# Adjacent heads in the two partition halves, with whole-tile loads of q, k and v and first-layer weights loaded by blocks of 32 partitions

## The chip, the cores and the metric

The kernel runs on one core of one Trainium2 chip. The metric is the device time of one execution in microseconds (us), lower is better. Engine names are those of the profile: PE is TensorE (matmul), PEld its weight loads, DVE VectorE, ACT ScalarE, POOL GpSimd, SP SyncE. SP, ACT and POOL can issue DMAs.

## What is computed

Attention with normalised q and k, and behind it a two-layer MLP with a leaky activation.

```python
# q, k, v: (8, 12, 448, 64) float32;  g_q, g_k: (64,)
def rmsnorm(x, g):
    return x / np.sqrt(np.mean(x * x, axis=-1, keepdims=True) + 1e-06) * g
q_n, k_n = rmsnorm(q, g_q), rmsnorm(k, g_k)
scores = q_n @ k_n.transpose(0, 1, 3, 2) / np.sqrt(64)
attn = np.exp(scores - scores.max(axis=-1, keepdims=True))
attn = attn / (attn.sum(axis=-1, keepdims=True) + 1e-09)
attn_out = attn @ v
x = attn_out.transpose(0, 2, 1, 3).reshape(8 * 448, 12 * 64)   # 3584 x 768
h = x @ w_in                                                   # w_in 768 x 2048
g = np.maximum(h, 0) + alpha * np.minimum(h, 0)
out = g @ w_out                                                # w_out 2048 x 768
```

## The kernel before

**Steps.** The 12 heads of a batch are laid out as two halves of the 128 partitions: g = 0 on partitions 0 to 63, g = 1 on 64 to 127. A partition holds J = 7 consecutive rows of the sequence for each head (64 x 7 = 448). A step y handles two heads of each half, so four heads; three steps (G = 3) make a batch, and 24 steps the kernel. Before the change half g holds heads 6g to 6g + 5, so that the four heads of a step are two neighbours and two other neighbours six heads away.

**Load and normalise.** `load_qk(y)` loads q and k of a step into two float32 tiles `nat` of 128 partitions x 2 heads x 448 values, each with one DMA for each half (L125). All go through SP, but for the second halves of steps 0 and 1, which ACT issues. For step 1 a copy on ACT into the tile (L123) keeps the load back. Steps 2, 5 and 8 load into a part of the tile `arena`. `square` (POOL, L180), `reduce` (DVE, L188) and `root` (ACT, L198 and L199) give the reciprocal root mean square, `scale` (DVE in the first steps, POOL from the k of step 3 on, L208) multiplies it in and makes a float16 tile `qs`. `follow` is a one-element copy on POOL (L282) that makes POOL wait for a scaling on DVE. `turn`, `turn_one` and, from step 7 on, `turn_dma` (SP, L307) transpose to `qT` and `kT`; PE does it in the early steps (L333). Step 0 is done in pieces (the `part_` functions), head by head for the squares of q. Ahead of its transposes PE runs a fixed number of dummy matmuls (`spin`, L765).

**Attention.** `score` (PE, L360) makes a tile of scores, `soft` (ACT, L374) exponentiates it to `expT`; `den` sums over keys by matmuls with ones, `attv` multiplies with v. The float16 tile `vt` holds v of a batch, loaded by `load_v` with one casting DMA for each half from POOL's queue (L134). In `attv` the 64 values of a head are taken as two sets of 32 columns: before the change the even and the odd ones. So block i of the transposed attention output `xT[:, g, i]` holds, on four groups of 32 partitions, 32 values each of four heads (i = 0 the even, i = 1 the odd ones of the first two steps), and for the third step 32-value groups of its two heads (i = 2).

**MLP.** `up` (PE, L499) multiplies a 128-column tile of `w_in_sb` with `xT`, six blocks (2 halves x 3) for each of 16 tiles; ACT (L539) and DVE (L543) apply the activation, and `down` (L561) and the `quad` functions (L626), which do four products with seven by sums and differences of blocks, make the output. `w_in_sb[:, block, :]` must hold the rows of w_in in the order in which `xT` holds its values. `load_w_in(c)` casts a quarter of the columns (512) for the blocks i = 0 and 1 with one DMA for each half, each over 128 partitions (L144), and, for even c, two quarters of the blocks i = 2 with two DMAs of 64 partitions (L151). It is called four times, at fixed places of POOL's queue among the squares and scalings of steps 2 to 5. `load_w_out` is called four times behind it (L158).

**Order.** The order of the work on each engine is written out by hand: a list of bursts of score tiles, with the functions `at` and `after` that put a job before or behind a burst, and a table that spreads `up`, `down` and `quad` units over the bursts. Nothing is reordered at run time: an engine that waits holds up all that is queued behind it. Waits for tiles are put in by the framework from what each instruction reads and writes.

Of the kernel before, what the change touches and what calls it, by code (L numbers as in the profile page):

```python
# [21 lines left out]
def kernel(  # L22
# [12 lines left out]
    nc = tc.nc  # L35
# [4 lines left out]
    J = S // 64  # L40
    HH = H // 2
    G = HH // 2
# [5 lines left out]
    FB = DF // 4  # L48
# [15 lines left out]


    q4, k4, v4 = (
        t.rearrange("b (g h) (p j) d -> b g p h (j d)", g=2, j=J) for t in (q, k, v)
    )
    out4 = out.rearrange("(b p j) m -> b j p m", b=B, j=J)

# [13 lines left out]
    w_in_sb = cst.tile([128, KM, DF], FP16, name="w_in_sb", tag="w_in_sb")  # L84
# [13 lines left out]
    def lent(start, size):  # L98

        return arena[:, start // 4 : (start + size) // 4]  # L100
# [5 lines left out]
    nat, sqs, qs, ss_t, rr_t, qkT, vt, xT = {}, {}, {}, {}, {}, {}, {}, {}  # L106
    SRC = {"q": q4, "k": k4}
# [4 lines left out]
    def load_qk(y, hold=False):  # L112
        b, i = divmod(y, G)
        for nm in "qk":
            if y in (2, 5, 8):
                t = lent(HB + "qk".index(nm) * NB4, NB4).rearrange(
                    "p (h j d) -> p h j d", h=2, j=J
                )
            else:
                t = ld.tile([128, 2, J, D], FP32, name="nat", tag="nat", bufs=4)  # L120
            if hold and nm == "q":

                nc.scalar.copy(out=t[:, 0, 0, 0:1], in_=expb)  # L123
            for g in range(2):
                (nc.scalar if y < 2 and g else nc.sync).dma_start(  # L125
                    out=t[ds(64 * g, 64)].rearrange("p h j d -> p h (j d)"),
                    in_=SRC[nm][b, g, :, ds(2 * i, 2)],
                )
            nat[y, nm] = t

    def load_v(b):
        t = att.tile([128, HH, J, D], FP16, name="vt", tag="vt", bufs=1)
        for g in range(2):
            nc.gpsimd.dma_start(  # L134
                out=t[ds(64 * g, 64)].rearrange("p h j d -> p h (j d)"), in_=v4[b, g]
            )
        vt[b] = t

    def load_w_in(c):

        src = moe_w_in[:, ts(c, FB)].rearrange("(g r) f -> g r f", g=2)
        dst = w_in_sb[:, :, ts(c, FB)].rearrange("p (g i) f -> p g i f", g=2)
        for g in range(2):
            nc.gpsimd.dma_start(  # L144
                out=dst[:, g, 0:2], in_=src[g, :256].rearrange("(p e) f -> p e f", e=2)
            )
        if c % 2 == 0:
            src = moe_w_in[:, ts(c // 2, 2 * FB)].rearrange("(g r) f -> g r f", g=2)
            dst = w_in_sb[:, :, ts(c // 2, 2 * FB)].rearrange("p (g i) f -> p g i f", g=2)
            for e in range(2):  # L150
                nc.gpsimd.dma_start(  # L151
                    out=dst[ds(64 * e, 64), :, 2],
                    in_=src[:, 256:].rearrange("g (p e) f -> e p g f", e=2)[e],
                )

    def load_w_out(c):
        oh, half = divmod(c, 2)
# [192 lines left out]
    def pre(ys):  # L350
        return len(ys) == 1 and ys[0] >= PRE and ys[0] % G == G - 1
# [27 lines left out]
    def over_keys(accs, ys, weights):  # L379

        heads = [(y, par, c) for y in ys for c in range(3 - len(ys)) for par in range(2)]
        for j in range(J):
            for n, (y, par, c) in enumerate(heads):
                for g in range(2):
                    nc.tensor.matmul(  # L385
                        out=accs[g][ds(32 * n, 32), :S],
                        lhsT=weights(g, y, par, c, j),
                        rhs=expT[y][ds(64 * g, 64), j, par, :],
                        start=(j == 0),
                        stop=(j == J - 1),  # L390
                    )

    def halved(ys):

        return len(ys) == 1 and ys[0] not in (2,)
# [48 lines left out]
    def attv(ys, half, spare=False, jobs=(), put=None, early=False):  # L444

        b, i = divmod(ys[0], G)
        v2 = vt[b].rearrange("p h j (d e) -> p h j d e", e=2)

        def weights(g, y, par, c, j):
            h = 2 * (y - G * b) + par  # L450
            return v2[ds(64 * g, 64), h, j, :, half if len(ys) == 2 else c]

        if half:
            av, accs = None, [psf.tile([128, 512], FP32, name="avb", tag="mm") for _ in range(2)]
        else:
            pool, tag = (pss, "sc") if spare else (psa, "acc")
            av = pool.tile([128, 2, 512], FP32, name="av", tag=tag)
            accs = (av[:, 0], av[:, 1])
        over_keys(accs, ys, weights)
        for f in jobs:  # L460
            f(ys)
        if b not in xT:
            xT[b] = att.tile([128, 2, G, S], FP16, name="xT", tag="xT")
        x, r = xT[b][:, :, i + half, :], rden[ys]
        if half:
            for g in range(2):
                nc.vector.tensor_mul(out=x[:, g], in0=accs[g][:, :S], in1=r[:, g])
        else:
            parts = [(x, av[:, :, :S], r)]
            if halved(ys):  # L470
                parts = [
                    (x[ds(64 * e, 64), :, c], av[ds(64 * e, 64), :, c], r[ds(64 * n, 64)])
                    for n, c in enumerate(ts(n, S // 2) for n in range(2)) for e in range(2)
                ]
            if put is not None:
                soon = 2 if early else 0
                muls(parts[:soon])
                put.append((muls, (parts[soon:],)))
            else:
                muls(parts)  # L480

    def muls(parts):
        for x, av, r in parts:
            nc.vector.tensor_mul(out=x, in0=av, in1=r)  # L484
# [10 lines left out]
    def up_part(hT, b, ft, lo, hi):  # L495

        for i in range(lo, hi):
            for g in range(2):
                nc.tensor.matmul(  # L499
                    out=hT[:, :S],  # L500
                    lhsT=w_in_sb[:, g * G + i, ts(ft, 128)],
                    rhs=xT[b][:, g, i, :],
                    start=(i == 0 and g == 0),
                    stop=(i == G - 1 and g == 1),
                )
# [274 lines left out]
    while m < NG * J or steps:  # L780
        n = len(bursts)
        while steps:
            ys, values = steps[0]
# [18 lines left out]
        while len(bursts[n]) < limit and m < NG * J:  # L802
            y, j = divmod(m, J)
# [29 lines left out]
    for y in range(G, NG):  # L833

        early = y < G + 2
        if early:
            n = turn_at[y - 1] + 1
        elif y == G + 2:
            n = den_at[G - 1]
        elif y == 2 * G:  # L840
            n = turn_at[y] - 4
        elif y % G == 1:
            n = den_at[y - 4] - 1 - pre((y - 2,))
        elif y % G:
            n = den_at[y - G] - pre((y - G,))
        else:
            n = av_at[y - 4]
        low = y > 3 * G + 1
        if low:
            nexts[root_at[y - 2]] = y  # L850
        elif y in (3 * G - 1, 3 * G):

            after(den_at[G] - (y < 3 * G), load_qk, y)
        else:
            at(n - (6 if early or y % G == G - 1 and pre((y - G,)) else 3 if y == 2 * G else 4 if y < 3 * G else 5), load_qk, y)
# [9 lines left out]
        if y == 3 * G:  # L865
            after(n, *jobs[n].pop()[:1], y, "k")
        roots[root_at[y]] = y
    at(av_at[G] - 6, load_v, 1)
    for b in range(2, B):
        after(av_at[G * b - 1] + 1, load_v, b)  # L870
# [116 lines left out]
    for n, g in enumerate((g_q, g_k)):  # L987
        for h in range(2):
            nc.gpsimd.dma_start(
                out=rows[NF + n : NF + n + 1, ds(64 * h, 64)], in_=g.unsqueeze(0)  # L990
# [12 lines left out]
    for h in range(2):  # L1003
# [13 lines left out]
        out=gain, in0=cols[:, NF : NF + 1], in1=cols[:, NF + 1 : NF + 2]  # L1017
# [3 lines left out]
    part_copy("q", full, nc.vector)  # L1021
    part_copy("k", lo, nc.vector)
    load_v(0)
    part_scale("k", hi, J - K0, nc.vector)
    follow(0, "k")
# [22 lines left out]
    for n in range(NB):  # L1048
# [6 lines left out]
        for t in first_tiles:  # L1055
            if t == (0, J - 2):
                spin(1)
            elif t == (1, J - 3):
                spin(2, False)
            elif t == (1, J - 2):  # L1060
                spin(1, False)
            elif t == (0, J - 1):
                turn_one(1, "q")
            elif t == (1, 0):
                turn_one(1, "k")
            elif t == (1, J - 1):
                turn(2)
            score(*t)
            if n == den_at[G - 1] - 1 and t == tiles[-1]:
                begin(0)  # L1070
                begin(1)
            elif lead and t == tiles[0]:
                soft(*t)
                den(dens[n])
                attv(avs[n], 0, True, (log, invert))
            elif lead and t == tiles[1]:
                begin(2)
# [26 lines left out]
        if n in avs and not lead and not sums:  # L1104

            for half in (1, 0) if avs[n] == (0, 1) else (0,):
                attv(avs[n], half)
# [11 lines left out]
        if n in roots:  # L1119
            y = roots[n]  # L1120
# [43 lines left out]
        for k, (f, a) in enumerate(gaps[n]):  # L1164
# [5 lines left out]
            else:  # L1170
                f(*a, spare)
                done += 1
                if n in jobs and not (lead and done < 5) and (
                    n < av_at[2 * G - 1] or done % 2
                ):
                    g, c = jobs[n].pop(0)
# [3 lines left out]
                while late and done == late[0][0]:  # L1180
                    _, g, c = late.pop(0)
# [51 lines left out]
```

## Time and profile before

| | |
|---|---|
| Median of 3 runs | 416.07 us (415.39 to 417.27) |
| The profiled execution | 418.46 us, its span 416.7 us |
| PE busy | 398.8 us (96%) |
| POOL busy | 255.8 us (61%) |
| DVE, ACT busy | 266.0 us, 257.6 us |
| DMA queue q1 (SP) | 53520 packets, 39.54 MB |
| DMA queue q0 (POOL) | 13472 packets, 11.81 MB |
| DMA queue q10 (ACT) | 976 packets, 1.31 MB |
| HBM read, written | 45.62 MB, 11.01 MB |

| DMA issues | count | KB each | us from issue to landing, median |
|---|---|---|---|
| q halves into nat, SP | 40 | 224.0 | 4.5 |
| k halves into nat, SP | 40 | 224.0 | 5.4 |
| q and k halves into arena, SP | 6 and 6 | 224.0 | 8.1 and 8.3 |
| q and k halves into nat, ACT | 2 and 2 | 224.0 | 5.2 and 6.8 |
| v halves, POOL | 16 | 336.0 | 8.4 |
| w_in, POOL | 12 | 256.0 | 9.4 |
| w_out, POOL | 4 | 768.0 | 10.5 |

A row of a timeline has the start in us from the span's start, the duration, the engine, the line, the operation, what is written and read, the count, and in brackets the idle time of the engine ahead of it with what ended it. "issue" in brackets is a wait that the profile shows no releaser for. POOLq and SPq are the issuing sides of these engines. In a DMA view, the share of a queue is the time that its packets took, as a share of 16 DMA engines over the stretch; it can pass 100% where packets overlap on an engine. Bytes are those written, so a casting load from float32 to float16 reads twice as many.

### The profile page before, as it was taken

What the parts mean: (1) busy time and instruction counts of PE and PEld (TensorE: products, weight loads), DVE (VectorE), ACT (ScalarE), POOL (GpSimd) and SP (SyncE); (2) the same over time, 40 slices, a digit from 0 to 9 for tenths busy, and PEclk for the clock granted to TensorE, in tenths of its full rate; (3) what the DMA queues carried; (4) which work ended last, traced back from release to release, by engine and by line L of the source; (5) the groups of instructions that cost most, each with busy time, mean ns of one, the idle gap of its engine ahead of it and who ended that gap; (6) DMA issues with size and microseconds to landing.
All of it is one profiled execution on the core that took longest, in us unless ns stands there. A gap on an engine that the chain in (4) does not pass through costs nothing.

```text
span 416.7 us, 11767 instructions
## 1 busy us (share of the span) xinstructions
PE 398.8 (96%) x5055; PEld 208.2 (50%) x5055; DVE 266.0 (64%) x420; ACT 257.6 (62%) x390; POOL 255.8 (61%) x180
## 2 busy tenths in 40 slices
PE   8698999999998999989999999999999999999996
PEld 3344445444455445544455445544555445655664
DVE  3875775476564575794788685958576755465322
ACT  4896687667845686565775787775656784135110
POOL 6689695669587985787094748386633507400870
PEclk9999999999999999999999999999999999999999
DMA  8999999973927496929946596369522800320133
GB/s 179 231 237 232 182 214 150 227 189 67 177 44 189 105 162 106 173 62 191 154 69 165 116 202 143 86 147 194 98 56 52 138 3 21 77 58 0 37 95 96
DMA packets 68019, 53.39 MB, mean 128 GB/s; under 512 B 35568, under 2 KB 67456, under 8 KB 67968
## 3 DMA queue, kind: packets, MB, share of 16 engines
q1 hardware_dynamic: 53520, 39.54, 45.0%
q0 software_dynamic: 13472, 11.81, 19.4%
q10 hardware_dynamic: 976, 1.31, 1.3%
q8 instruction: 39, 0.64, 0.7%
q14 instruction: 12, 0.10, 0.1%
HBM read 45.62 MB, written 11.01 MB: 136 GB/s over the span
## 4 chain that ended last, share of the span: by engine, by line
PE 46%; DVE 7%; DMA 1%; ACT 0%; issue 0%; SPq 0%; DVEq 0%
PE hT L499 14%; PE hTa L499 7%; PE qx L626 5%; PE oq L626 3%; PE sc L360 3%; PE qc L626 3%; PE av L385 2%; PE qz L626 2%; PE oqm L626 2%; DVE ss L188 1%; PE avb L385 1%; PE oqa L626 1%; DVE xT L484 1%; PE dn L385 1%; DVE kT L318 1%; DMA out_dram<-osb 1%
## 5 line engine op out<-in xcount | busy, mean ns | idle before, releaser
L374 ACT ACTIVATE expT<-sc 128x896 f16<-128x896 f32 x168 | 147.8, 914 | 53.2 <-PE sc L360 53.0
L499 PE MATMUL hT<-xT,w_in_sb 128*128 128x448 f16 x546 | 113.6, 353 | 3.5 <-issue 2.3
L499 PEld LDWEIGHTS <-w_in_sb 128*128 128x128 f16 x768 | 72.9, 98 | 77.9 <-issue 13.5
L543 DVE TENSOR_TENSOR gT<-hT,gT 128x448 f16<-128x448 f32 x91 | 56.7, 623 | 41.3 <-ACT gT L539 40.5
L208 POOL TENSOR_TENSOR qs<-nat,rr 128x896 f16<-128x896 f32 x36 | 61.0, 1713 | 34.8 <-issue 22.3
L539 ACT ACTIVATE gT<-hT,cols 128x448 f16<-128x448 f32 x90 | 57.1, 635 | 36.1 <-PE hT L499 35.9
L180 POOL TENSOR_TENSOR sq<-nat 128x896 f32<-128x896 f32 x32 | 53.6, 1683 | 39.7 <-DMA nat<-in_q_dram 30.4
L360 PE MATMUL sc<-qT,kT 64*32 64x448 f16 (+1 forms) x1092 | 52.9, 356 | 4.4 <-ACT expT L374 1.9
L626 PEld LDWEIGHTS <-gT 128*128 128x128 f16 x352 | 33.5, 98 | 26.8 <-issue 5.7
L499 PE MATMUL hTa<-xT,w_in_sb 128*128 128x448 f16 x210 | 45.5, 352 | 0.0
L188 DVE TENSOR_REDUCE ss<-sq 128x14 f32<-128x896 f32 (+1 forms) x37 | 38.5, 1053 | 4.4 <-POOL sq L180 4.3
L484 DVE TENSOR_TENSOR xT<-av,rden 64x448 f16<-64x448 f32 (+1 forms) x37 | 27.2, 734 | 13.5 <-PE av L385 5.5
L539 ACT ACTIVATE gT<-hTa,cols 128x448 f16<-128x448 f32 x35 | 22.3, 637 | 18.9 <-PE hTa L499 18.9
L543 DVE TENSOR_TENSOR gT<-hTa,gT 128x448 f16<-128x448 f32 x35 | 21.8, 624 | 18.1 <-ACT gT L539 18.0
L360 PEld LDWEIGHTS <-kT 64*32 64x32 f16 (+1 forms) x1092 | 15.6, 93 | 35.1 <-issue 29.3
L561 PE MATMUL op<-w_out_sb,gT 128*128 128x384 f16 x160 | 27.6, 327 | 1.0 <-issue 1.0
L385 PEld LDWEIGHTS <-vt 64*32 64x32 f16 x1344 | 20.2, 92 | 13.5 <-issue 4.3
L561 PEld LDWEIGHTS <-gT 128*128 128x128 f16 x192 | 17.9, 98 | 14.8 <-issue 3.8
L614 POOL TENSOR_TENSOR gs<-gT 128x1024 f16<-128x1024 f16 x3 | 6.4, 2123 | 30.4 <-DVE gT L543 28.1
L385 PE MATMUL av<-expT,vt 64*32 64x448 f16 x896 | 24.3, 350 | 0.3 <-DVE osb L674 0.3
L622 POOL TENSOR_TENSOR gT<-gT 128x1024 f16<-128x1024 f16 x11 | 23.4, 2126 | 0.0
L626 PE MATMUL qx<-w_out_sb,gT 128*128 128x384 f16 x120 | 20.8, 326 | 1.0 <-DVE rden L428 1.0
(148 smaller groups left out, 492.6 us busy)
## 6 DMA issues: line engine op xcount, KB each, us to landing
out_dram<-osb SPq DMA_DIRECT2D x107, 96.0 KB, 3.0
nat<-in_q_dram SPq DMA_DIRECT2D x40, 224.0 KB, 4.5
nat<-in_k_dram SPq DMA_DIRECT2D x40, 224.0 KB, 5.4
vt<-in_v_dram POOLq DMA_DIRECT2D x16, 336.0 KB, 8.4
w_in_sb<-in_moe_w_in_dram POOLq DMA_DIRECT2D x12, 256.0 KB, 9.4
w_out_sb<-in_moe_w_out_dram POOLq DMA_DIRECT2D x4, 768.0 KB, 10.5
arena<-in_q_dram SPq DMA_DIRECT2D x6, 224.0 KB, 8.1
arena<-in_k_dram SPq DMA_DIRECT2D x6, 224.0 KB, 8.3
```

The costliest lines, as they stand in the source:

```text
L180: nc.gpsimd.tensor_mul(out=sqf[:, c], in0=src[:, c], in1=src[:, c])
L188: nc.vector.tensor_reduce(out=o[:, c], in_=sqs[y, nm][:, c], axis=AXIS_X, op=ALU.add)
L208: eng.tensor_mul(out=t.rearrange("p j h d -> p h j d"), in0=nat[y, nm], in1=rr_t[y][:, "qk".index(nm)].unsqueeze(3).broadcast_to((128, 2, ...
L360: nc.tensor.matmul(out=sc[ds(64 * g + m * c, m), par, :S].rearrange("p (j c) -> p j c", j=J), lhsT=kT[ds(64 * par, 64), j, g, ts(c, m)], r ...
L374: nc.scalar.activation(out=expT[y][:, j], in_=scs[y, j][:, :, :S], func=AF.Exp, scale=QK_SCALE, bias=EXP_BIAS,)
L385: nc.tensor.matmul(out=accs[g][ds(32 * n, 32), :S], lhsT=weights(g, y, par, c, j), rhs=expT[y][ds(64 * g, 64), j, par, :], start=(j == 0), ...
L484: nc.vector.tensor_mul(out=x, in0=av, in1=r)
L499: nc.tensor.matmul(out=hT[:, :S], lhsT=w_in_sb[:, g * G + i, ts(ft, 128)], rhs=xT[b][:, g, i, :], start=(i == 0 and g == 0), stop=(i == G ...
L539: nc.scalar.activation(out=g, in_=hT[:, :S], func=AF.Copy, scale=alpha_sb[:, ft : ft + 1])
L543: nc.vector.tensor_max(out=g, in0=hT[:, :S], in1=g)
L561: nc.tensor.matmul(out=op[:, :OH], lhsT=gT[:, ft, ts(tile % J, 128)], rhs=w_out_sb[:, ft, ts(oh, OH)], start=(ft == 0), stop=(ft == NF - 1),)
L626: nc.tensor.matmul(out=bank[:, c], lhsT=g[:, ft], rhs=v[:, ft, c], start=(first and ft == 0), stop=(ft == HF - 1), skip_group_check=True,)
```

## The change

Half g now holds the heads of parity g: the four heads of a step are four neighbours in memory, and partition and half together are one dimension of 128 with one stride. With that, q and k of a step are one DMA each over 128 partitions, all on SP's queue (q of step 0 in two, one for each head index), and v of a batch is one DMA. `attv` takes the first and the second 32 values of a head and no longer the even and odd ones. The rows of w_in follow: `w_in_sb` holds blocks 0 to 3 (i = 0 and 1 of both halves) and 4, 5 (i = 2), which `block_of` numbers; for each group of 32 partitions one DMA loads its rows, four for blocks 0 to 3 of each quarter of the columns, and four for blocks 4 and 5 of each half of the columns: 24 DMAs in all where there were 12.

```diff
@@ -64,7 +64,7 @@
 
 
     q4, k4, v4 = (
-        t.rearrange("b (g h) (p j) d -> b g p h (j d)", g=2, j=J) for t in (q, k, v)
+        t.rearrange("b (h g) (p j) d -> b (g p) h (j d)", g=2, j=J) for t in (q, k, v)
     )
     out4 = out.rearrange("(b p j) m -> b j p m", b=B, j=J)
 
@@ -121,37 +121,34 @@
             if hold and nm == "q":
 
                 nc.scalar.copy(out=t[:, 0, 0, 0:1], in_=expb)
-            for g in range(2):
-                (nc.scalar if y < 2 and g else nc.sync).dma_start(
-                    out=t[ds(64 * g, 64)].rearrange("p h j d -> p h (j d)"),
-                    in_=SRC[nm][b, g, :, ds(2 * i, 2)],
-                )
+            o = t.rearrange("p h j d -> p h (j d)")
+            for h in range(2) if (y, nm) == (0, "q") else (slice(0, 2),):
+                nc.sync.dma_start(out=o[:, h], in_=SRC[nm][b, :, ds(2 * i, 2)][:, h])
             nat[y, nm] = t
 
     def load_v(b):
         t = att.tile([128, HH, J, D], FP16, name="vt", tag="vt", bufs=1)
-        for g in range(2):
+        nc.gpsimd.dma_start(out=t.rearrange("p h j d -> p h (j d)"), in_=v4[b])
+        vt[b] = t
+
+    def block_of(g, i):
+        return 2 * g + i if i < 2 else 4 + g
+
+    def load_w_in(c):
+
+        src = moe_w_in[:512].rearrange("(n x p) f -> n p x f", n=4, p=32)
+        for n in range(4):
             nc.gpsimd.dma_start(
-                out=t[ds(64 * g, 64)].rearrange("p h j d -> p h (j d)"), in_=v4[b, g]
-            )
-        vt[b] = t
-
-    def load_w_in(c):
-
-        src = moe_w_in[:, ts(c, FB)].rearrange("(g r) f -> g r f", g=2)
-        dst = w_in_sb[:, :, ts(c, FB)].rearrange("p (g i) f -> p g i f", g=2)
-        for g in range(2):
-            nc.gpsimd.dma_start(
-                out=dst[:, g, 0:2], in_=src[g, :256].rearrange("(p e) f -> p e f", e=2)
+                out=w_in_sb[ds(32 * n, 32), :4, ts(c, FB)], in_=src[n, :, :, ts(c, FB)]
             )
         if c % 2 == 0:
-            src = moe_w_in[:, ts(c // 2, 2 * FB)].rearrange("(g r) f -> g r f", g=2)
-            dst = w_in_sb[:, :, ts(c // 2, 2 * FB)].rearrange("p (g i) f -> p g i f", g=2)
+            w = ts(c // 2, 2 * FB)
+            src = moe_w_in[512:].rearrange("(n g e p) f -> e n p g f", n=2, g=2, e=2)
             for e in range(2):
-                nc.gpsimd.dma_start(
-                    out=dst[ds(64 * e, 64), :, 2],
-                    in_=src[:, 256:].rearrange("g (p e) f -> e p g f", e=2)[e],
-                )
+                for n in range(2):
+                    nc.gpsimd.dma_start(
+                        out=w_in_sb[ds(64 * e + 32 * n, 32), 4:, w], in_=src[e, n, :, :, w]
+                    )
 
     def load_w_out(c):
         oh, half = divmod(c, 2)
@@ -444,11 +441,11 @@
     def attv(ys, half, spare=False, jobs=(), put=None, early=False):
 
         b, i = divmod(ys[0], G)
-        v2 = vt[b].rearrange("p h j (d e) -> p h j d e", e=2)
+        v2 = vt[b].rearrange("p h j (e d) -> p h j e d", e=2)
 
         def weights(g, y, par, c, j):
             h = 2 * (y - G * b) + par
-            return v2[ds(64 * g, 64), h, j, :, half if len(ys) == 2 else c]
+            return v2[ds(64 * g, 64), h, j, half if len(ys) == 2 else c]
 
         if half:
             av, accs = None, [psf.tile([128, 512], FP32, name="avb", tag="mm") for _ in range(2)]
@@ -498,7 +495,7 @@
             for g in range(2):
                 nc.tensor.matmul(
                     out=hT[:, :S],
-                    lhsT=w_in_sb[:, g * G + i, ts(ft, 128)],
+                    lhsT=w_in_sb[:, block_of(g, i), ts(ft, 128)],
                     rhs=xT[b][:, g, i, :],
                     start=(i == 0 and g == 0),
                     stop=(i == G - 1 and g == 1),
```

## The prediction, made before the changed kernel ran

> **What bounds the kernel now.** I read the page first: which engine is full, and in which slices.
>
> ```profile
> PE 398.8 (96%) x5055; PEld 208.2 (50%) x5055; DVE 266.0 (64%) x420; ACT 257.6 (62%) x390; POOL 255.8 (61%) x180
> ...
> PE   8698999999998999989999999999999999999996
> ...
> DMA  8999999973927496929946596369522800320133
> ```
>
> TensorE (PE) is busy 398.8 of 416.7 us, so 17.9 us of idle time is all that faster transfers can give back. The windows place it: 8.35 us before 50 us (41.65 busy), 5.5 us from 50 to 400, 4.0 us behind that. DMA is dense (9) in the first seven slices of 10.4 us. In that front POOL squares and scales q and k and, between these, issues the loads of v and of the weights; so POOL's timeline comes next.
>
> ```profile
> 18.49 1.68 POOL L180 TENSOR_TENSOR sq<-arena 128x896 f32<-128x896 f32 x1
> 20.11 1.48 POOL L144 DMA_DIRECT2D w_in_sb<-in_moe_w_in_dram  x2
> 21.59 1.22 POOL L151 DMA_DIRECT2D w_in_sb<-in_moe_w_in_dram  x2
> 24.08 0.19 POOL L282 COPY mark<-qs 128x1 f16<-128x1 f16 x1 [1.27 <-DVE qs L208]
> 24.22 3.46 POOL L180 TENSOR_TENSOR arena<-nat 128x896 f32<-128x896 f32 x3
> 27.63 1.46 POOL L144 DMA_DIRECT2D w_in_sb<-in_moe_w_in_dram  x2
> 29.11 2.42 POOL L208 TENSOR_TENSOR arena<-nat,rr 128x896 f16<-128x896 f32 x1
> ...
> 45.48 3.33 POOL L208 TENSOR_TENSOR qs<-nat,rr 128x896 f16<-128x896 f32 x2 [3.34 <-ACT rr L199]
> ```
>
> POOL hardly rests from 18 us on: its slack is 1.27 us before 24.08 and 3.34 us before 45.48. The second exists because PE itself stood still; PE's timeline:
>
> ```profile
> 42.47 0.92 PE L499 MATMUL hT<-xT,w_in_sb 128*128 128x448 f16 x4 [2.34 <-issue]
> ...
> 49.29 0.95 PE L333 MATMUL tps<-ident,qs 128*128 128x128 f16 x14
> ```
>
> The 2.34 us are the longest PE stall. Nothing on chip ends it: xT was done at 39.97, and the c=0 weights had landed by 34.9. What does end near it is a block of 16,384 bytes on the instruction queue, moved from 39.70 to 41.01. Such blocks come every 252 recorded PE instructions; this one came some 200 too late by that count, and the one at 130.98 some 220, before PE's next long stall. I read both as instructions kept back by crowded DMA engines. How crowded, the DMA view of two stretches tells:
>
> ```profile
> DMA packets 290, 0.46 MB, mean 230 GB/s; under 512 B 32, under 2 KB 290, under 8 KB 290
> ...
> q1 hardware_dynamic: 288, 0.46, 107.8%
> ```
> ```profile
> q0 software_dynamic: 450, 0.50, 73.6%
> q1 hardware_dynamic: 286, 0.45, 40.5%
> ```
>
> First 12 to 14 us, where q1 (the q and k halves) runs alone: 288 packets take 107.8% of 16 engines for 2 us, 120 ns each. Then 31 to 35 us, beside the weights: 40.5% of 16 x 4 us over 286, 91 ns. Alone they are slower than in company, so the half-loads hinder one another. Single packets of 1,792 bytes span 74 ns (5th percentile) to 166 ns; at 74 ns, 16 engines would move 387 GB/s.
>
> Last, 130 to 139 us, the one place behind the front where a late load reaches PE:
>
> ```profile
> 130.30 1.68 POOL L180 TENSOR_TENSOR sq<-nat 128x896 f32<-128x896 f32 x1 [2.79 <-DMA nat<-in_q_dram]
> ...
> 133.68 3.42 PE L561 MATMUL op<-w_out_sb,gT 128*128 128x384 f16 x20 [0.99 <-issue]
> ...
> 138.19 1.11 PE L499 MATMUL hT<-xT,w_in_sb 128*128 128x448 f16 x5 [0.59 <-DVE osb L572]
> ```
>
> POOL's squares wait for q, DVE's reduction (134.03) for POOL, the xT products (135.03 to 137.55) and the osb copy stand behind it on DVE, and PE waits 0.59 us for that copy.
>
> **The change part by part.** *q and k loads.* Two DMAs of 64 partitions become one of 128. A pair is 917,504 bytes: 4.0 us at the 230 GB/s shown, 2.4 us at 387. I take the latter, since 91 ns is already seen in company; the other bound is no gain.
>
> The Trainium skill, page "SBUF — State Buffer", section "Door 1: The DMA port swizzle (why [64,N] ≈ [32,N])", says that partitions 0 to 63 reach only 8 of 16 ports, some 218 GB/s, and all 128 reach twice that. The 230 GB/s agree with it; by its 436 GB/s a pair would take an estimated 2.1 us, which leaves the sum as it is. It also speaks against the other half of the change, as 32 partitions reach 8 ports too; the trace shows the weights written at 204 GB/s on 128 partitions (56 to 60 us), so by the rule the pieces would hardly be slower.
>
> *Issues on SP and ACT.* A half-load costs SP 0.60 us with 128 runs, an output with 64 runs 0.61, so I price a whole load at 0.6 too (at most 1.2, the two it replaces). ACT loses four issues (0.63 to 0.86 us) before 5.3 us. The first q lands sooner, but no score comes sooner: PE's spins run to 9.19 and the transposes behind them set the first score at 11.04. Worth 0 on the path.
>
> *Front of POOL.* k of step 1 no longer keeps POOL back at 12.55: it starts at 11.8, behind the copy of 11.65, and all that hangs on it is 0.75 us earlier; the square of 18.49 ends near 19.35.
>
> *w_in.* 12 issues become 24. The nearest row for 32 partitions x 4 runs is L151 with as many runs (64 x 2): 0.62 us; the g loads with 16 runs took 0.49, L144 with 256 runs 0.73. I take 0.60, ends 0.49 and 0.73. Then: c=0, 8 x 0.60, ends at 24.15 (marker copy 24.3, against 24.22 before: the 1.27 us of slack and the 0.75 are used up). Squares to 27.75; c=1 (4 x 0.60 for 1.46) to 30.15; scale of k to about 31.85 (1.7, as elsewhere; in the row above DVE stretched it to 2.42). PE transposes this k from about 32.3, so nothing is lost. Squares to 35.15, c=2 to 39.95, squares to 43.3, c=3 to 45.7, scale of step 4 to 49.0. PE without its 2.34 us stall would reach step 4's transposes at 46.95, does q's, and waits for k until 49.05; before, k's seven began at about 49.77. **Front: -0.7 us.** Ends: -2.3 (0.49 us an issue: POOL in time) and +2.4 (0.73: c=0 to 25.2, c=3 to 48.8, k scaled at 52.1). What hid the old issues was POOL's slack; now it is gone, and PE's recovered time with it.
>
> *v.* One issue of 768 runs for two of 0.69: between 0.73 and the 0.94 of a w_out issue with 1,024; about 0.5 us less POOL time a batch, beside full PE: 0.
>
> *Steady stage.* From 50 to 130 us PE has no stall over 0.25 us, so there is nothing to gain. At 125.6 the pair lands (data from 127.0) by 129.8 and not 132.16: POOL's two squares end at 132.1 instead of 133.99, xT 1.8 us sooner, and the 0.59 us go; the instruction block meets 2.4 us of load and not 5, so the 0.99 goes. **-1.6 us** (ends 0 and -1.6). The stalls at 179.5 (0.98) and 186.6 (0.32) have DVE full for microseconds ahead of them: 0, ends ±1.0. At 215.5 (0.64): 0 or -0.6.
>
> *Weight layouts.* v's columns become contiguous, block numbers of w_in change: loads of vt (stride 2) take 92 ns, of contiguous kT 93, under the matmuls: 0.
>
> Sum: -0.7 - 1.6 = -2.3 us. The profiled execution took 418.46 us (span 416.7 and 1.8 around it) and becomes 416.2; the median of the runs, 2.4 us lower, becomes 413.8, 0.55% less. About 0.5%, 2.1 us, is what a measurement of this kernel can tell from no change, so this forecast lies just beyond it.
>
> **The rivals.** *One: POOL's eight slots, slower.* The DMA records show POOL's loads on eight semaphores (111 to 118) in turn, and on SP that a ninth load waits for the first: the k load of 6.95 starts when semaphore 104 fills at 6.94, 0.7 us after the issue before it. With 24 weight loads, c=1 waits for the landing of c=0's first four. It decides once a landing exceeds 8.4 us (27.75 - 19.35). Now they take 8.0 to 12.7. At 11.0, the L151 median: c=1 issued to 32.75, c=2 43.75, c=3 51.15, scale 54.5, so +4.8: 420.9; at 9.4, +1.6. Against it: those landings are long because v's load, issued at 9.33, lands only at 23.8 ahead of c=0, and with quicker q and k that queue should be empty at 19.
>
> *Two: hidden anyway.* POOL gives back all the front saves, and PE, 96% busy, merely meets its next engine wait: 415.0 to 417.0. For it: the front's order is fixed, and POOL's slack is only 4.6 us against some 6 us of added issues. Against it: the stall at 138.19.
>
> *Three: the load does not get quicker* (the packets stay at 120 ns, bound by the memory they read). Then the instruction stalls stay, and POOL's issues with 0 to +2 remain: 416.0 to 418.5. Against it: 91 ns beside other traffic that reads more in all.
>
> **How the numbers follow.** Forecast 0.44 (412.0 to 415.0), hidden 0.28, slots 0.17, not quicker 0.11. Of the forecast's cases nearly all, and a few of the hidden ones, lie under 414.0: faster 0.47. Slots is slower in most of its range, not quicker in some: slower 0.22. Same 0.31. The forecast's low end adds what the bounds allow (-2.3, -1.6 and half of the -1.6 at 179 to 216: 411.4); above, 418.5 takes in rivals two and three and the mild half of one.
>
> **What would show it.** Right: q1 packets near 75 to 90 ns where they run alone; no PE stall at 40 to 42 and at 132 to 138; POOL without idle time from 18 to 60 us; PE waiting some 2 us at L333 near 47. Rival one: gaps between POOL's L144 successors. Wrong altogether: w_in issues over 0.75 us, or new DVE and POOL waits behind 140 us of more than 2 us.

## The result, and the profile after

The changed kernel takes 412.50 us (median of 8 runs, 411.96 to 414.78), the kernel before on the same chip 416.04 us (8 runs, 414.04 to 418.80): the ratio is 0.9916, 95% interval 0.9887 to 0.9946. A second series on another chip gave 412.51 (7 runs) against 416.57 (12 runs), 0.9903 (0.9862 to 0.9944). So it is faster by 3.5 to 4.1 us, where 2.3 were forecast. The profiled execution of after happens to be the slowest of its series: 414.78 us, span 413.0. A second profile, of an execution near the median (412.52 us, span 410.7), is among the experiments, as is a second one of before (416.39 us, span 414.6).

The page of after, the same three rows as before:

```profile
PE 398.9 (97%) x5055; PEld 208.1 (50%) x5055; DVE 266.9 (65%) x420; ACT 257.3 (62%) x390; POOL 255.8 (62%) x184
...
PE   7889999899999999999999999999999999999996
...
DMA  8999899957754894329861697279332700320143
```

PE does the same 398.9 us of work in a shorter span. What is gone is idle time: 14.1 us are left of 17.9. DMA is still dense in the front, but a whole load of 448 KB now lands in about the time that a half-load took (median 4.9 us for q and 5.4 for k, against 4.5 and 5.4). Stretches of after's DMA view, 6 to 8 us, where q1 runs nearly alone, and then 31 to 35 us (per queue: packets, MB, share of 16 engines):

```profile
DMA packets 459, 0.68 MB, mean 342 GB/s; under 512 B 78, under 2 KB 459, under 8 KB 459
...
q1 hardware_dynamic: 408, 0.68, 99.5%
```
```profile
q0 software_dynamic: 514, 0.46, 78.5%
q1 hardware_dynamic: 214, 0.37, 31.1%
```

Alone, 408 packets fill 99.5% of 16 engines for 2 us: 78 ns each, against 120 before, and 342 GB/s are written, not 230. In company (31 to 35 us) it is 93 ns, no better than the 91 before. Over the whole execution the 1,792-byte packets of q1 have a median of 74 ns (122 before).

POOL's timeline in the front (start, duration; in brackets the idle time ahead):

```profile
19.98 2.21 POOL L141 DMA_DIRECT2D w_in_sb<-in_moe_w_in_dram  x4
22.19 2.13 POOL L149 DMA_DIRECT2D w_in_sb<-in_moe_w_in_dram  x4
24.61 0.19 POOL L279 COPY mark<-qs 128x1 f16<-128x1 f16 x1 [0.29 <-DVE qs L205]
...
30.36 1.70 POOL L205 TENSOR_TENSOR arena<-nat,rr 128x896 f16<-128x896 f32 x1
...
45.06 3.35 POOL L205 TENSOR_TENSOR qs<-nat,rr 128x896 f16<-128x896 f32 x2
```

A weight issue takes 0.55 us (L141) or 0.53 (L149). The only idle time that POOL's timeline shows between 18.4 and 48.3 us is 0.29 us, so POOL sets the pace there, as forecast, and scales step 4 from 45.06 where the old order had 45.48. PE's timeline behind it:

```profile
42.48 1.30 PE L496 MATMUL hT<-xT,w_in_sb 128*128 128x448 f16 x6
...
47.37 0.56 PE L330 MATMUL tps<-ident,qs 128*128 128x128 f16 x7
48.47 0.56 PE L330 MATMUL tps<-ident,qs 128*128 128x128 f16 x7 [0.54 <-POOL qs L205]
```

The stall of 2.34 us ahead of hT is gone, and half a microsecond of it is paid back at step 4's transposes. Two other waits stand out in this profile: one at `ct`, the small matmul ahead of the first transposes that turns the loaded rows of g and alpha into columns, for the loads of g_k, and one at 75 us with no releaser:

```profile
9.84 0.20 PE L995 MATMUL ct<-ident,arena 18*128 18x18 f32 x1 [1.28 <-DMA arena<-in_g_k_dram]
...
75.68 0.75 PE L382 MATMUL avb<-expT,vt 64*32 64x448 f16 x20 [0.99 <-issue]
```

Neither is altogether new. Before waits at `ct` in its second profile, and for a short time in the same `avb` matmuls in both (the row of the first is shown; 0.27 us in the second):

```profile
8.89 0.20 PE L998 MATMUL ct<-ident,arena 18*128 18x18 f32 x1 [0.75 <-DMA arena<-in_g_k_dram]
```
```profile
76.33 0.57 PE L385 MATMUL avb<-expT,vt 64*32 64x448 f16 x15 [0.24 <-issue]
```

Both kernels have 5,055 matmuls in one order, so I set the k-th of the one against the k-th of the other. How much later (+) or earlier (-) after gets there, in us, for the first pair of profiles and for the pair of second profiles:

| up to | forecast | first pair | second pair |
|---|---|---|---|
| first score (11 us) | 0 | +0.54 | +0.51 |
| behind step 4's transposes (50 us) | -0.7 | -1.22 | -0.91 |
| 82 us | -0.7 | -0.47 | -1.54 |
| 141 us | -2.3 | -2.28 | -2.12 |
| 174 us | -2.3 | -2.46 | -2.56 |
| 190 us | -2.3 | -3.50 | -3.83 |
| the end | -2.3 | -3.59 | -3.84 |

The sum up to 174 us lies near the forecast, but partly by luck: in the first pair a front that gained 0.5 us more than forecast is paid back by the stall at 75 us, and in the second 1.1 of the 2.56 us come from places where nothing was forecast (50 to 82 and 141 to 174 us). The step between 174 and 190 us was not in the forecast.

### The profile page after: what moved, and what is told of

Same layout as the page of the kernel before. It is cut to its first block, busy times and chain, and to the rows that moved or that the text cites. A ratio compares the mean times of both kernels' runs of the same rounds, so it can differ in the third digit from the quotient of the medians.

```text
span 413.0 us, 11724 instructions
## 1 busy us (share of the span) xinstructions
PE 398.9 (97%) x5055; PEld 208.1 (50%) x5055; DVE 266.9 (65%) x420; ACT 257.3 (62%) x390; POOL 255.8 (62%) x184
## 4 chain that ended last, share of the span: by engine, by line
PE 49%; DVE 6%; ACT 0%; issue 0%; DVEq 0%
PE hT L496 14%; PE hTa L496 7%; PE qx L623 5%; PE sc L357 3%; PE oq L623 3%; PE qc L623 3%; PE qz L623 2%; PE av L382 2%; PE oqm L623 2%; PE avb L382 1%; PE dn L382 1%; PE oqa L623 1%; DVE ss L185 1%; DVE xT L481 1%; DVE kT L315 1%; PE qza L623 1%
## 5 line engine op out<-in xcount | busy, mean ns | idle before, releaser
L382 PEld LDWEIGHTS <-vt 64*32 64x32 f16 x1344 | 20.2, 92 | 14.1 <-issue 5.0
```

The lines of the kernel that those rows point to most:

```text
L382: nc.tensor.matmul(out=accs[g][ds(32 * n, 32), :S], lhsT=weights(g, y, par, c, j), rhs=expT[y][ds(64 * g, 64), j, par, :], start=(j == 0), ...
```

## The experiments

The theory: the gain comes from packets that take 75 to 90 ns once a q or k load spans 128 partitions, with the front's stall and the late load at 130 us gone. Rivals: it comes from the number or the engine of the issues, or from the order in memory; or the weights' extra issues take it back.

**Halves and bands.** Both keep all of after but the shape of q and k loads, with the same number of DMAs in each: two of 64 partitions, or two of 128 partitions with one head index each.

```diff
-            for h in range(2) if (y, nm) == (0, "q") else (slice(0, 2),):
-                nc.sync.dma_start(out=o[:, h], in_=SRC[nm][b, :, ds(2 * i, 2)][:, h])
+            for g in range(2):                       # halves
+                p = ds(64 * g, 64)
+                nc.sync.dma_start(out=o[p], in_=SRC[nm][b, p, ds(2 * i, 2)])
+            for h in range(2):                       # bands
+                nc.sync.dma_start(out=o[:, h], in_=SRC[nm][b, :, ds(2 * i, 2)][:, h])
```

Halves:

> The changed kernel, but each load of q and k is two DMAs of 64 partitions again, both on SP; heads adjacent, v and w_in as in the change. Theory 'width': a half-load is slow because its packets hinder one another, and the crowded DMA engines keep instruction blocks and squares late. Then 1,792-byte packets go back from a median of 74 ns to about 120, the PE stall near 40 us comes back (1 to 2.4 us), so do those near 132 to 138 (1.6) and 179 (1.0), and the time is 415.0 to 417.5 us. Rival 'neighbours': the gain is from the four heads of a step lying together in memory; then packets stay under 90 ns and the time at 412.2 to 413.2.

Bands:

> The changed kernel, but each load of q and k is two DMAs over 128 partitions, one for each head index: as many DMAs and bytes each as in the kernel before. Theory 'width': packets stay at a median of 74 ns, no stall comes back, 412.0 to 413.3 us. Rival 'issues': the gain is from half as many DMAs and half the issue time on SP; then part of it goes, 413.8 to 416.

On one chip halves took 416.19 us (12 runs; ratio to before 0.9978, 0.9949 to 1.0008) and bands 412.71 (6 runs; 0.9896, 0.9855 to 0.9938). Median packets: 119 ns and 74 ns. DMA views from 12 to 14 us, halves first:

```profile
q1 hardware_dynamic: 300, 0.48, 109.6%
```
```profile
q0 software_dynamic: 321, 0.29, 87.8%
q1 hardware_dynamic: 136, 0.21, 33.3%
```

That is 117 ns a packet alone, against 78 even beside the weights. The width of the transfer carries the gain; neighbours in memory, issues all on SP, and the whole load of v are in both kernels and are not enough. The Trainium skill, page "DMA: Bandwidth & Descriptors", section "Rules for kernel authors", advises against splitting a transfer over the two partition halves because they serialize, sharing the same engines. The runs agree with the advice, with 3.5 us of 416 between the two splits; but the two DMAs of bands share the engines as well and lose nothing, so that reason is not the one seen here.

The time of halves came out as expected, but not where it was to be lost. Its profile has 0.40 us at the place of the 2.34, where 1 to 2.4 were expected, and no stall at 132 to 138 or at 179 us. PE waits elsewhere, for a DVE copy and for POOL:

```profile
33.66 0.56 PE L331 MATMUL tps<-ident,arena 128*128 128x128 f16 x7 [0.91 <-DVE qT L338]
...
41.76 0.92 PE L497 MATMUL hT<-xT,w_in_sb 128*128 128x448 f16 x4 [0.40 <-DMA w_in_sb<-in_moe_w_in_dram]
...
50.02 0.57 PE L331 MATMUL tps<-ident,qs 128*128 128x128 f16 x7 [0.88 <-POOL qs L206]
```

About 1.4 of the 3.3 us that this execution (414.89 us) takes longer than the profiled one of bands (411.56) are lost while the granted clock was 0.50, for 3.41 us from 20.7, which bands' did not have. The medians do not hang on that: the executions at a granted clock of 0.998 or more have 415.87 (5 of halves) and 412.37 (4 of bands). So the runs show that the width is worth some 3.5 us; where a typical execution of halves loses them, this one profile does not show.

In halves POOL also has to wait to issue weights, in its timeline at c = 1:

```profile
29.81 0.55 POOL L142 DMA_DIRECT2D w_in_sb<-in_moe_w_in_dram  x1 [0.60 <-DMA w_in_sb<-in_moe_w_in_dram]
31.34 0.55 POOL L142 DMA_DIRECT2D w_in_sb<-in_moe_w_in_dram  x1 [0.98 <-DMA w_in_sb<-in_moe_w_in_dram]
```

**The weights in twelve DMAs.** After, with each w_in load over 128 (or 64) partitions again. The rows of w_in then stand in the wrong order, so what is timed is not the reference's product.

```diff
-        for n in range(4):
+        for g in range(2):
             nc.gpsimd.dma_start(
-                out=w_in_sb[ds(32 * n, 32), :4, ts(c, FB)], in_=src[n, :, :, ts(c, FB)]
+                out=w_in_sb[:, ds(2 * g, 2), ts(c, FB)],
+                in_=moe_w_in[ds(256 * g, 256), ts(c, FB)].rearrange("(p x) f -> p x f", x=2),
             )
...
```

> The changed kernel with w_in loaded in 12 DMAs of 128 and 64 partitions, as many and as large as before the change; the rows of w_in are then in the wrong order for the blocks. Theory 'POOL pays': the 12 added issues take 24 x 0.545 - 8.3 = 4.8 us of POOL, which show as PE waiting at the transposes of step 4 (0.54 us, and a quarter of the shift lost there); without them that wait goes and the time is 411.6 to 412.0 us. Rival 'covered': something else sets the place of these transposes, and the time stays at 412.3 to 412.8.

It took 411.94 us (6 runs; 0.9894, 0.9849 to 0.994). POOL scales step 4 from 43.03 and PE waits for it no more. The extra issues thus cost the wait at step 4's transposes, about half a microsecond; the medians alone, 411.94 and 412.5, do not separate the two kernels.

**The weights in 24 DMAs, without the rest.** The kernel before, with each w_in load cut in two.

```diff
-            nc.gpsimd.dma_start(
-                out=dst[:, g, 0:2], in_=src[g, :256].rearrange("(p e) f -> p e f", e=2)
-            )
+            for m in range(2):
+                p = ds(64 * m, 64)
+                nc.gpsimd.dma_start(
+                    out=dst[p, g, 0:2],
+                    in_=src[g, ds(128 * m, 128)].rearrange("(p e) f -> p e f", e=2),
+                )
...
```

> The kernel before with nothing changed but w_in's 12 DMAs cut into 24 (blocks of 64 and of 32 partitions). Theory 'POOL pays': about 5 us more on POOL against its slack of 1.27 and 3.34 us, so its scaling of step 4 ends 1 to 3 us later and PE waits for it; ratio to the kernel before 1.002 to 1.007. 'Slots': with slow q and k loads the c=1 pieces wait for the landing of c=0's first four, POOL stands still for some us near 28 and 41, ratio 1.008 or more. Rival 'covered': 0.999 to 1.001.

It took 419.21 us (12 runs; 1.0079, 1.0051 to 1.0107), 0.8% slower than before. POOL's timeline at c = 1, and PE's behind it:

```profile
29.19 0.58 POOL L146 DMA_DIRECT2D w_in_sb<-in_moe_w_in_dram  x1 [0.75 <-DMA w_in_sb<-in_moe_w_in_dram]
30.69 0.58 POOL L146 DMA_DIRECT2D w_in_sb<-in_moe_w_in_dram  x1 [0.92 <-DMA w_in_sb<-in_moe_w_in_dram]
```
```profile
34.63 0.56 PE L337 MATMUL tps<-ident,arena 128*128 128x128 f16 x7 [2.50 <-POOL arena L212]
...
49.63 0.56 PE L337 MATMUL tps<-ident,qs 128*128 128x128 f16 x7 [0.52 <-POOL qs L212]
...
51.27 0.56 PE L337 MATMUL tps<-ident,qs 128*128 128x128 f16 x7 [1.07 <-POOL qs L212]
```

This is rival one at work: the second group of weight issues waits for landings of the first, POOL's scale comes late, PE stands. With slow loads of q and k ahead of them the 24 DMAs cost more here than they do in after. Not every kernel with slow loads shows this price: halves has 24 w_in DMAs behind half-loads too and stays at 0.9978, with 0.91 us where PE waits 2.50 here.

**v in halves.** After, with v as two DMAs of 64 partitions.

> The changed kernel with v of a batch as two DMAs of 64 partitions, as before the change. Theory: the v load is covered, POOL pays 0.5 us a batch off the path: 412.2 to 413.0 us. Rival 'width for v too': its packets hinder one another, v lands later and PE waits for it or for instructions: 413.2 to 414.5.

413.59 us (10 runs; 0.9935, 0.9902 to 0.9968). This lies in the range of the rival, 413.2 to 414.5, but its interval holds the ratio of after, and its profile has no PE wait for v; its longest is 1.92 us at `ct`, for g_k. So nothing is shown for the single load of v, either way.

**A crowd on the queues.** After, with eight more loads of 64 partitions, 224 KB each, on SP from 32.5 us, into a part of the w_out tile that is overwritten later.

```diff
+    unused = w_out_sb.rearrange("p f m -> p (f m)").bitcast(FP32)
+
+    def load_crowd():
+        for s in range(4):
+            for g in range(2):
+                p = ds(64 * g, 64)
+                nc.sync.dma_start(
+                    out=unused[p, ds(2 * s * J * D, 2 * J * D)].rearrange(
+                        "p (h c) -> p h c", h=2
+                    ),
+                    in_=q4[B - 1, p, :2],
+                )
+
+    at(9, load_crowd)
```

> The changed kernel with eight more transfers of 64 partitions (229 KB each) behind step 6's load on SP, from about 32.5 us on, into a part of the weight tile that is loaded over later. Nothing computed waits for them. Theory 'instructions': crowded DMA engines bring the block of instructions due at 36 us only at 39 or later, and PE stands still for 1 to 2.5 us near 40.5 although xT and the weights are there; part of it is covered by the 0.54 us wait at step 4's transposes, so 413.0 to 414.8 us. Rival: the stall of the kernel before had another cause; then PE shows no gap over 0.3 us from 39 to 44 and the time is 412.3 to 412.8 us.

418.02 us (10 runs; 1.0029, 0.9997 to 1.0061), over the 413.0 to 414.8 expected: the whole gain is lost again. PE's timeline, then POOL's:

```profile
44.68 1.61 PE L496 MATMUL hT<-xT,w_in_sb 128*128 128x448 f16 x4 [3.54 <-DMA w_in_sb<-in_moe_w_in_dram]
```
```profile
45.84 0.54 POOL L141 DMA_DIRECT2D w_in_sb<-in_moe_w_in_dram  x1 [1.67 <-DMA w_in_sb<-in_moe_w_in_dram]
47.60 0.54 POOL L141 DMA_DIRECT2D w_in_sb<-in_moe_w_in_dram  x1 [1.22 <-DMA w_in_sb<-in_moe_w_in_dram]
```

The stall of before is back at its old place, and longer. The profile puts it down to a load of w_in, but none fits: the weights of c = 1 had all landed by 38.93, and of those of c = 2 the second load lands only at 45.55 and the last after 49, when these matmuls have long run. What fits is the block of 16,384 bytes on the instruction queue: it started at 41.49, about 198 recorded PE instructions late, and its move took 1.3 us. In before it was 197 late for a stall of 2.34 us, in after 10 early with no stall. The place fits too. All these stalls, the 0.40 us of halves included, are at the same matmul, 955 recorded PE instructions (matmuls and weight loads) from the start, and the stall at 75 us is at 1,711: that is 756 later, three blocks of 252. Each ends 1.4 to 1.9 us after its block has landed (42.80 and 44.68 here). What is argued, and not shown by a run of its own, is that PE had run out of instructions there.

The stall is not all of the loss. Matched with after's second profile, PE loses 3.7 us at it and another 1.6 right behind it, where the granted clock was 0.50 for 3.41 us from 44.8 (four of these matmuls took 1.61 us and not 0.92). POOL's last group of weight issues waits for landings, as in rival one.

**Loads of g from ACT.** In after all of q and k for steps 0 to 2 are issued by 4.6 us, since ACT's copy that holds step 1 back runs at 2.04 instead of 3.49 (ACT has no loads left to issue ahead of it). The small loads of g, from POOL, land behind them: 6.1 us after their issue (g_k), 4.9 before. In the five profiles in which SP has issued these loads by 4.2 to 4.6 us, g_k lands at 9.7 to 10.2; in halves and bands, which have the early copy too but issue until 8.7 and 7.4 us, at 8.2 and 9.0. Here ACT issues the loads of g ahead of its table load.

```diff
-    nc.scalar.preload_act_table_set("natural_log_exp_and_others")
-    nc.gpsimd.dma_start(out=rows[:NF], in_=moe_alpha.rearrange("(t p) -> t p", p=128))
     for n, g in enumerate((g_q, g_k)):
         for h in range(2):
-            nc.gpsimd.dma_start(
+            nc.scalar.dma_start(
                 out=rows[NF + n : NF + n + 1, ds(64 * h, 64)], in_=g.unsqueeze(0)
             )
+    nc.scalar.preload_act_table_set("natural_log_exp_and_others")
+    nc.gpsimd.dma_start(out=rows[:NF], in_=moe_alpha.rearrange("(t p) -> t p", p=128))
```

> The changed kernel with the four small loads of g_q and g_k issued from ACT ahead of its table load, no longer from POOL behind the identity matrices. Theory 'late gains': the 1.28 us for which PE waits at 9.84 us are these loads queued behind three steps of q and k; then the small matmul follows the spins at 8.6 us, the first score comes at 10.4 to 10.8 instead of 11.58, and 0.5 to 1.2 us are left at the end: 411.3 to 412.0. Rival: POOL's queue gives the lead back before 50 us, 412.3 to 412.8.

410.63 us (6 runs; 0.9854, 0.9813 to 0.9895), less than the 411.3 to 412.0 expected. The wait ahead of ct is gone and the first score comes at 10.20 us instead of 11.58:

```profile
8.43 0.23 PE L995 MATMUL ct<-ident,arena 18*128 18x18 f32 x1
8.60 0.73 PE L256 MATMUL tps<-ident,qs 128*128 128x128 f16 x10
10.20 0.57 PE L357 MATMUL sc<-qT,kT 64*64 64x448 f16 x8 [0.88 <-DVE kT L266]
```

The edit does two things at once: it issues the loads of g earlier and from another engine, and ACT's copy is late again (3.43 us), so that q of step 1 is issued at 3.65 us and not at 2.25. Which of the two brings the gain is not separated.

**And the last weight load later.** The same, with `load_w_in(3)` put behind burst 10 instead of 8.

> The kernel gains_act, with the last four loads of w_in (c=3) moved behind the scaling of step 4 on POOL. Theory 'POOL pays': PE's wait for POOL at step 4's transposes (0.37 us in gains_act) goes and a little more, since k is scaled 2.2 us sooner: 409.8 to 410.4 us. Rival: c=3 now lands too late for tiles 12 to 15 or something else is next: 410.5 to 411.2.

411.19 us (6 runs; 0.9882, 0.9842 to 0.9922), on another chip than the version without the move: the rival's range, not the 409.8 to 410.4 of the theory. Step 4's transposes wait no more; a wait of 0.48 us for DVE at 53 us takes the place. The first score comes at 11.05 us in this profile, so its place varies by about a microsecond between executions.

**All on one chip.** Copies of before, of after and of the last two versions, unchanged and profiled again.

Before:

> The kernel before, unchanged, profiled a second time. Theory: three of its long PE stalls are not one thing. The 0.59 us at 138 comes from a late load of q at 127 (half-loads, packets of some 120 ns) and should be there again, with POOL's square waiting over 2 us for q. The instruction stalls (2.34 us at 40 to 42, 0.99 at 133) should come back, at about the same places, since the DMA engines are crowded there in every execution; 1 to 2.5 us each. The 0.98 at 179.5 was put down to a late square on POOL beside a sum of two tiles on DVE; two kernels with half-loads (the changed kernel with halves, and the one before with 24 weight loads) do not show it, so it should be absent as often as present: if it is absent here, it is no effect of the change. Rival: all four are fixed places of this kernel and come again within 0.2 us.

After:

> The changed kernel, unchanged, profiled a second time on the chip of the two versions beside it. Theory: the wait for the small loads of g ahead of the first transposes (ct, 1.29 us in the profile of after) and the wait of 0.54 us for POOL at step 4's transposes are set by the order of the queues and come again, 1 to 1.9 us and 0.4 to 0.7 us; the stall of 0.99 us at 75 is an instruction block that happened to come late in that one execution and need not come again. Median 412.0 to 413.5 us. Rival: the stall at 75 is a new cost of the changed order and is there again.

Loads of g from ACT:

> The version with the loads of g issued from ACT, now on one chip with the changed kernel and with the version that also moves the last weight load. Theory: 1.5 to 2 us below the changed kernel, 410.3 to 411.2 us, because PE waits no more for ct and the first score comes at 10.2 instead of 11.6 us. Rival: the difference seen before was one of chips, and it lies within 0.5 us of the changed kernel.

And the weight load moved:

> The version with the loads of g from ACT and the last weight load moved behind burst 10. Theory: the 0.37 to 0.5 us wait at step 4's transposes goes, but the last columns of the first layer's weights land later and a wait in the MLP may take its place (0.48 us at 53 in its first profile): within 0.5 us of the version without the move, 410.3 to 411.5 us. Rival: the wait in the MLP was a coincidence, and it is 0.4 us faster than the version without the move.

| | median, us | runs | ratio to before | first score, us |
|---|---|---|---|---|
| after | 412.51 | 7 | 0.9903 (0.9862 to 0.9944) | 11.77 |
| loads of g from ACT | 410.82 | 6 | 0.9852 (0.9805 to 0.9899) | 9.80 |
| weight load moved too | 410.83 | 6 | 0.9854 (0.9812 to 0.9896) | 10.26 |

The loads of g from ACT are worth 1.7 us beyond the change; moving the last weight load adds nothing, as expected: the new wait, again 0.48 us, is as long as the old.

The stall at 75 us does not come again in after's second profile, but stands in the second one of the version with g on ACT, 1.09 us at the same instruction. In both profiles that show it the instruction block is 125 recorded instructions late, in after's second profile 5. So it comes and goes between executions of the changed order. In before's two profiles the block is 93 late, and PE loses 0.6 us at the next few of these matmuls. The wait ahead of ct came again with 0.69 us, less than the 1 to 1.9 expected, and the wait at step 4's transposes with 0.38 instead of 0.54.

In the second profile of before the instruction stalls come again at their places, but shorter, 1.76 us at 40 and 0.41 at 132. I had expected 1 us and more of each. The 0.59 us at 138 did not come again, although POOL's square waits 2.61 us for q as before: that late load reaches PE in one execution and not in the other. And the stall behind 178 us, which I held for a coincidence of one execution, is there again, longer:

```profile
179.45 1.79 PE L626 MATMUL qx<-w_out_sb,gT 128*128 128x384 f16 x10 [1.28 <-DVE rden L428]
```

## Why the prediction was right, and where it was not

**The load's price** was right: 74 to 78 ns and 342 GB/s alone, against 74 and 387 in the sum. Halves and bands show that the width does it. Rival three falls with them.

**The front** was right in mechanism: stall gone, POOL the pace, PE waiting at step 4's k. Its size was -1.22 and -0.91, not -0.7, and several terms were off. A w_in issue was taken at 0.60 us and took 0.55 and 0.53, so step 4 was scaled by 48.41 and not 49.0. PE's wait there was 0.54 (0.38) us and not about 2. POOL's lead of 0.75 us at the square of 18.49 came to 0.13 (18.36): k of step 1 no longer held POOL back, but a scaling on DVE did, until 12.19. Against them stands the start: "no score comes sooner" was true, but the 0 hid a loss. The prediction counted ACT's four issues as relief and did not follow what the earlier hold copy lets through: q and k of steps 1 and 2 ahead of g_k. The first score came 0.5 us later in both pairs, and the version that issues the loads of g from ACT gained 1.7 us.

The second pair's -0.91 also holds the granted clock. In 8 of the 14 profiles it was 0.50 once for 3.41 us between 11 and 25 us. In before's second profile this began at 11.7 us and in after's at 21.0; matched matmul by matmul, PE lost about 1.0 us by it in before and 1.4 in after.

**130 to 139 us**: -1.6 forecast, -1.8 and -0.6 measured between 82 and 141 us. The load is early now; PE's timeline of after runs through:

```profile
130.09 5.37 PE L558 MATMUL op<-w_out_sb,gT 128*128 128x384 f16 x32
135.39 0.57 PE L357 MATMUL sc<-qT,kT 64*32 64x448 f16 x16
135.89 1.31 PE L496 MATMUL hT<-xT,w_in_sb 128*128 128x448 f16 x6
```

But the 0.59 and most of the 0.99 were of the one profiled execution, and the step priced them as if every one had them.

**"The stalls at 179.5 and 186.6 have DVE full ahead of them: 0"** is the step that failed: 174 to 190 us gave -1.0 and -1.3. DVE was full because POOL held it up. DVE's two sums stand ahead of the copy to `rden` for which PE waits at `qx`, the first product of a quad. They are, in before's first profile, its second, and after's first:

```profile
177.49 1.87 DVE L614 TENSOR_TENSOR arena<-gT 128x1024 f16<-128x1024 f16 x1
179.46 0.69 DVE L615 TENSOR_TENSOR arena<-arena,gT 128x1024 f16<-128x1024 f16 x1
```
```profile
176.05 0.96 DVE L614 TENSOR_TENSOR arena<-gT 128x1024 f16<-128x1024 f16 x1
177.11 1.98 DVE L615 TENSOR_TENSOR arena<-arena,gT 128x1024 f16<-128x1024 f16 x1
```
```profile
175.03 0.68 DVE L611 TENSOR_TENSOR arena<-gT 128x1024 f16<-128x1024 f16 x1
175.81 0.69 DVE L612 TENSOR_TENSOR arena<-arena,gT 128x1024 f16<-128x1024 f16 x1
```

POOL's second square ran from 177.13 to 178.81 in the first; it ends 0.55 us before the long sum does. In the second profile the two squares end at 176.46 and 178.55, again 0.55 and 0.54 us before the two long sums end. In after the squares are over at 174.87. In both profiles of before the first square had waited for q's load, 2.71 and 2.15 us; in after it waits for a reduction on DVE and no longer for the load. Of the 14 profiles of this study only the two of before have the overlap at these two sums, and only they have PE's stall at qx; in the twelve others the two sums take 0.68 and 0.69 us and start 0.05 to 0.16 us behind the squares. Among these are two with half-loads, before with 24 weight DMAs (whose square also waits for q, 2.25 us) and halves. So quicker loads of q take the squares out of the sums' way, but they are not the only thing that does, and no run moves the squares alone. A long sum alone is no stall either: the pair of sums before this one, at 157 to 161 us in after, takes 1.59 and 2.06 us beside a scaling on POOL (0.69 each in before), and PE does not wait there. The Trainium skill, page "SBUF — State Buffer", section "Who interferes with whom", says that a DVE instruction with two SBUF inputs blocks fully against a GpSimd one that reads SBUF, whichever starts second. The durations agree with it: the wait until the square's end, and then the rest.

**Rivals.** One (slots) is a real mechanism, as halves, the crowd and before with 24 DMAs show, and did not decide because w_in landings fell to a median of 5.0 us, under the 8.4 from which it begins. Two (hidden) was wrong in the amount: POOL gave back about half a microsecond, and the time lies under its 415.0.

**Still open:** halves and before with 24 DMAs differ by 1% relative to before, though both load q and k by halves and w_in in 24 pieces; which of the other edits makes that is not separated. And why a block comes late in one execution and not in the next is not shown; with eight more loads it did, but in after the block of 75 us was late once and in time once with the same loads.

## What to carry to other kernels

Before pricing a transfer, look at its packets where it runs alone and again in company: if they are slower alone, the transfer's own shape limits it, and a load over all 128 partitions may mend it. When an edit takes work off an engine, follow what that engine was holding back: here a copy that ran 1.5 us sooner let large loads out ahead of a few small ones that the first transposes needed. And where an engine is full ahead of a stall, compare the duration of each instruction there with the same instruction elsewhere in the trace: a sum at 1.87 us instead of 0.68 was the sign that the stall could move.

## What the runs showed of the hardware that was not expected

- SP's issue of a k load over 128 partitions (256 runs) took a median of 0.47 us in after, and one over 64 (128 runs) 0.6 us in before; twice the runs cost less. POOL's issues fell only a little with the runs: 0.73 us for 256, 0.55 for 128.
- With eight more half-loads in flight PE stood still for 3.54 us, though its data was there, and the profile named a weight load as the cause that was not needed. The stalls of this kind begin at recorded PE instruction 955 or 1,711, three blocks apart, and end 1.4 to 1.9 us after a block of instructions has landed.
- A sum of two tiles on DVE (0.68 us) that meets one of these POOL squares ends 0.54 to 0.55 us after the square, whatever is left of it: 0.96, 1.87 and 1.98 us were seen.
